# Issuing the y matmuls of a recurrence as two matmuls of 64 tokens each, in two column groups of the TensorE array

## The chip, the cores and the metric

One core of a Trainium2 chip runs the whole kernel. The metric is the device time of one execution in microseconds (us); the median of three runs of the kernel before is 934.26 us (932.96 to 934.57). TensorE multiplies matrices, VectorE and ScalarE work on vectors and evacuate results from PSUM, GpSimd does small jobs, and SyncE issues the transfers. A matmul here has a stationary operand, loaded into the array (its columns become the rows of the result), and a moving operand that is streamed through it.

## The reference, cut to what matters

```python
# 4 batches x 8 heads, 768 tokens, 48 features per head
for t in range(S):
    state = alpha[:, :, t, :, None] * state + np.einsum('bhd,bhe->bhde', k[:, :, t], v[:, :, t])
    y[:, :, t] = np.einsum('bhd,bhde->bhe', q[:, :, t], state)
# heads side by side: x is 3072 x 384
xn = x / sqrt(mean(x * x) + 1e-6) * rms_g
x = (silu(xn @ w_gate) * (xn @ w_val)) @ w_out          # d_ff = 1536
out = max(x @ w1, x @ w2, x @ w3) @ w_out2              # d_ff = 768
```

## The kernel before

The recurrence is cut into 24 tiles of 128 tokens of one batch: six chunks of four batches, so tiles 0 to 3 have no state yet, tiles 4 to 23 do, and tiles 20 to 23 are the last chunk, which leaves no state. Heads are treated in four pairs. For a tile, VectorE turns the inputs (in tiles 0 to 5 TensorE does), makes running products of alpha in a first half (`pre_br`) and in a second half (`pre_bq`), and writes kT, qT and the decayed state Sd. TensorE then forms the scores of each head (`pe_b`, line 643, two groups of rows of the array), VectorE masks them into `at`, and `pe_c` makes from them U, the tile's own contribution to the state (line 666), and y. U's two matmuls of a pair write partitions 0 to 47 and 64 to 111. y has a matmul with the state for both heads of a pair (line 673, 96 moving columns) and one with `at` for each head (line 678, 48 moving columns); each has all 128 tokens as columns of its stationary operand. All of these are float32, and each appears in the trace as two loads and two matmuls. Then y is normalized, turned (line 712) and split into two float32r halves, xh and xl.

The first MoE goes over the 3072 tokens in eight blocks of 384 (three tiles) and over the hidden layer in strips of 128: one block with one strip is a slot, and there are 96. A slot has a gate (`g`, line 756), an up-projection (`v`, line 756) and a down-projection (`s`, line 803), of nine matmuls of 128x384 each; VectorE multiplies the two (line 789, "the product" of the slot), which frees the PSUM bank for the next slot's up-projection, and splits the result (line 797). The first two blocks take turns, so that strips 0 to 5 of the weights are first used in slots 0 to 5, and strips 6 to 11 in slots 12 to 17. The weights are float64; VectorE joins their words (lines 57 to 59) and splits them in two (line 379), two chunks of 128x384 at a time. The second MoE follows; its weights are loaded once the last tile is through.

All of this is one program order, written by a planner (`Order`): each part has an engine, a cost, a due slot and parts that it needs, and the planner plays this through once, starting on each engine the due part that can start. What it writes per engine is then executed in that order. Until the first up-projection it adds fillers to TensorE where it expects rest, products that nothing uses (line 763). Each engine executes its own list in order and waits on semaphores for the others.

Of the kernel before, what the change touches and what calls it, by code (L numbers as in the profile page):

```python
# [37 lines left out]
# The upper word of a float64, read as a float32, grows with the number's magnitude. From  # L38
# 2**-119 to 2**121 it is in [LEAST, MOST).
# [6 lines left out]
def words(raw, n):  # L46
    """Upper words (as bits and as float32) and lower words of n float64s."""
    bits, floats = (raw.bitcast(t).rearrange("p (n w) -> p n w", w=2) for t in (I32, F32))
    return bits[:, :n, 1], floats[:, :n, 1], bits[:, :n, 0]


def join(nc, raw, t, n):
    """Float64 to float32 bits, in three steps: sign, exponent and the first 23 bits of the mantissa,
    the last of them set (its error is then as often up as down)."""
    up, _, low = words(raw, n)
    bits = t.bitcast(I32)
    yield nc.vector.tensor_scalar(bits, up, 3, TOP2 + 1, ALU.logical_shift_left, ALU.bitwise_or)
    yield nc.vector.scalar_tensor_tensor(bits, up, BELOW, bits, ALU.bitwise_or, ALU.bitwise_and)  # L58
    yield nc.vector.scalar_tensor_tensor(bits, low, 29, bits, ALU.logical_shift_right, ALU.bitwise_or)  # L59


def any_weight(nc, p, dst, src, n):
    """float64 to float32 of any magnitude: what is too small becomes 0, what is too large inf."""
    raw = p.tile([P, n], I64, name="aw_raw")
    nc.sync.dma_start(out=raw, in_=src)
    up, upf, low = words(raw, n)
    sq = p.tile([P, n], F32, name="aw_sq")
    nc.vector.tensor_tensor(sq, upf, upf, ALU.mult)
    small = p.tile([P, n], I32, name="aw_small")
    nc.vector.tensor_scalar(small, sq, LEAST * LEAST, -1.0, ALU.is_ge, ALU.mult)  # L70
    large = p.tile([P, n], I32, name="aw_large")
    nc.vector.tensor_scalar(large, sq, MOST * MOST, -1.0, ALU.is_ge, ALU.mult)
    e = p.tile([P, n], F32, name="aw_e")
    for _ in join(nc, raw, e, n):
        pass
    bits = e.bitcast(I32)
    nc.vector.tensor_tensor(bits, bits, small, ALU.bitwise_and)
    inf = p.tile([P, n], I32, name="aw_inf")
    nc.vector.tensor_scalar(inf, up, SIGN, 0x7F800000, ALU.bitwise_and, ALU.bitwise_or)
    nc.vector.copy_predicated(bits, large.bitcast(U32), inf)  # L80
    nc.vector.tensor_copy(dst, e)


def slow_path(ctx, tc, q, k, v, alpha, wg, wv, wo, g, w1, w2, w3, wo2, out, x_scr):
    """The recurrence as it stands, then both MoEs in float32 products."""
# [91 lines left out]
class Order:  # L177
    """The order in which the parts of the kernel are issued. Each part occupies one engine for
    about its cost and needs other parts done; of those that can start, the one due first does.
    Some hold PSUM banks until other parts are done."""  # L180

    SIGNAL = 0.1
    # The tensor engine runs at half its clock in a tick if fewer than ENOUGH columns left it in the last.
# [13 lines left out]
    def busy_tensor(self, t, cost, columns):  # L197
        """When the tensor engine, from t on, is through with what takes it cost at its full clock."""
        while cost > 1e-9:
            tick = int(t / self.TICK + 1e-9)  # L200
            slow = 1 if self.count.get(tick - 1, 0) >= self.ENOUGH else 2
            step = min(cost, ((tick + 1) * self.TICK - t) / slow)
            self.count[tick] = self.count.get(tick, 0) + columns * step / cost
            columns -= columns * step / cost
            cost -= step
            t += step * slow
        return t
# [73 lines left out]
def gla_moe_moe(ctx: ExitStack, tc: tile.TileContext, q, k, v, alpha, wg, wv, wo, g, w1, w2, w3, wo2, out):  # L281
# [35 lines left out]
    # LAT: from a load's issue until its data can be used; HEAD: slots by which the first chunks are ahead.  # L317
# [3 lines left out]
    class Weights:  # L321
        """Float64 weights loaded ahead, then cut into two float32r, two chunks at a time."""

        def __init__(self, tag, pool, bufs, chunks, where, due, needs):
            """chunks: source and shape; where(i): the two destinations; due(i): slot of first use."""
# [57 lines left out]
        def check(self, i):  # L383
            """Magnitudes outside of float32's normal range make sums that are too large."""
# [10 lines left out]
        def ready(self, i):  # L395
            """What has to be done before chunk i is used."""
            return (self.tag, "rest", i - i % 2)

# [1 line left out]
    # The first two blocks take turns, so that each weight is used twice as it comes.  # L400
# [54 lines left out]
    def take(n, rows, a, w):  # L455
        """A bank that nothing waits in, the one free for the longest."""
# [15 lines left out]
    # The tensor engine turns the operands of the first tiles, while the vector engine is the busier one.  # L472
    NPE = 6

    class Tile_:
        """One tile of 128 tokens."""

        def __init__(self, n):
# [4 lines left out]
            # Slots of the first MoE by which its parts are due: at + step * (0 to 4).  # L483
# [40 lines left out]
            add("pc", "PE", (2.57 if c else 1.72) + (0 if last else 0.5), 2.5,  # L524
# [12 lines left out]
        def load(self):  # L537
# [7 lines left out]
            # Partition 64 j + 32 u + t of an input's tile: tokens 4 t to 4 t + 3 of the heads of parity  # L545
            # j, from feature 32 u on (and, past a token's last feature, what nothing uses).
# [26 lines left out]
        def turn(self, dst, src):  # L573
            """Features to the partitions (those of a head to 0 to 47 or 64 to 111), tokens along them."""
# [12 lines left out]
        def pre_br(self):  # L587
            # R[s]: product of alpha after s; Q[t]: product up to t over the whole tile's.
            # One scan over the four pairs: a zero multiplier starts each anew.
# [70 lines left out]
        def pe_c(self):  # L660
            vt, at = self.vt, self.at
            if self.c < NC - 1:
                self.U, self.in_u = take(self.n, W, NP, D)
                for pr in range(NP):
                    for i, lo, hi in HALVES:
# [3 lines left out]
                        )  # L669
            self.y, self.in_y = take(self.n, P, H, D)  # L670
            for pr in range(NP):
                if self.c:
                    nc.tensor.matmul(  # L673
                        self.y[:, 2 * pr:2 * pr + 2, :].rearrange("p a d -> p (a d)"), self.qT[:, pr, :],
                        Sds[self.s][:, pr, :], start=True, stop=False, skip_group_check=True,
                    )
                for i in range(2):
                    nc.tensor.matmul(  # L678
                        self.y[:, 2 * pr + i, :], at[i][:, pr, :], vt[:, 2 * pr + i, :],
                        start=not self.c, stop=True, skip_group_check=True,  # L680
                    )
# [79 lines left out]
    def fill():  # L761
        """A product that nothing uses: the tensor engine's clock falls when it rests."""
# [231 lines left out]
    def flag():  # L994
        """1 if all operands were in the range of the chunked form and of the split weights."""
# [50 lines left out]
```

## Time and profile before

| | |
|---|---|
| median of the runs | 934.26 us (932.96 to 934.57) |
| span of the profiled execution, from its first to its last instruction | 932.6 us |
| TensorE busy with matmuls | 904.6 us, 97% of the span |
| TensorE busy with loads of stationary operands | 884.9 us, 95% |
| VectorE busy | 528.1 us, 57% |
| ScalarE busy | 352.5 us, 38% |

The page's time of the profiled execution is its span; the timed runs are told by the device and lie a little above. Loads run beside matmuls, so the first two shares overlap. The ends of matmuls are modelled, and one is drawn longer than its place in the stream: how long a run of them takes is read from start to start. The share of VectorE is an average: the page's 40 slices show it at eight or nine tenths and more from the second to the eighth and at three or less at the end.

### The profile page before, as it was taken

What the parts mean: (1) busy time and instruction counts of PE and PEld (TensorE: products, weight loads), DVE (VectorE), ACT (ScalarE), POOL (GpSimd) and SP (SyncE); (2) the same over time, 40 slices, a digit from 0 to 9 for tenths busy, and PEclk for the clock granted to TensorE, in tenths of its full rate; (3) what the DMA queues carried; (4) which work ended last, traced back from release to release, by engine and by line L of the source; (5) the groups of instructions that cost most, each with busy time, mean ns of one, the idle gap of its engine ahead of it and who ended that gap; (6) DMA issues with size and microseconds to landing.
All of it is one profiled execution on the core that took longest, in us unless ns stands there. A gap on an engine that the chain in (4) does not pass through costs nothing.

```text
span 932.6 us, 15178 instructions
## 1 busy us (share of the span) xinstructions
PE 904.6 (97%) x5910; PEld 884.9 (95%) x5910; DVE 528.1 (57%) x1052; ACT 352.5 (38%) x898; POOL 23.2 (2%) x70
## 2 busy tenths in 40 slices
PE   4899999999999999999999999999999999999997
PEld 3798999999999999999999999999999999999996
DVE  3989999987666666666666347556323323323221
ACT  3567777323233323233223258644212212212121
POOL 1000000000000000000000000000000000000000
PEclk9989999999999999999999999999999999999999
DMA  8746646343122122223221026321100101101000
GB/s 169 146 115 179 175 141 188 84 117 87 43 55 73 45 51 78 56 56 81 56 56 53 1 75 180 102 92 45 52 26 26 51 1 51 32 21 51 1 26 29
DMA packets 106238, 69.08 MB, mean 74 GB/s; under 512 B 49200, under 2 KB 103856, under 8 KB 106160
## 3 DMA queue, kind: packets, MB, share of 16 engines
q1 hardware_dynamic: 106160, 68.05, 27.5%
q8 instruction: 48, 0.79, 0.4%
q14 instruction: 30, 0.25, 0.1%
HBM read 57.41 MB, written 10.62 MB: 73 GB/s over the span
## 4 chain that ended last, share of the span: by engine, by line
PE 88%; DVE 5%; DMA 3%; issue 2%; ACT 1%; POOL 0%; SPq 0%; DVEq 0%; POOLq 0%; ACTq 0%
PE bank L756 53%; PE bank L803 15%; PE bank L956 8%; PE bank L678 4%; PE bank L673 2%; PE bank L643 2%; DMA raw<-in_moe_w_dram 2%; PE bank L666 1%; PE bank L712 1%; DVE cv_t L58 1%; PE bank L569 1%; DVE R L597 1%; PE bank L636 1%; PE bank L763 1%; DVE cv_t L59 1%
## 5 line engine op out<-in xcount | busy, mean ns | idle before, releaser
L941 DVE TENSOR_TENSOR sg<-sg,bank 128x384 f32<-128x384 f32 x96 | 53.1, 554 | 172.0 <-PE bank L756 165.6
L789 DVE TENSOR_TENSOR sg<-sg,bank 128x384 f32<-128x384 f32 x96 | 53.0, 552 | 107.8 <-PE bank L756 107.7
L793 ACT ACTIVATE hh<-sg 128x384 fp32r<-128x384 f32 x96 | 50.2, 523 | 144.0 <-DVE sg L789 144.0
L756 PE MATMUL bank<-xh,wgh 128*128 128x384 f32 x288 | 100.3, 348 | 0.0
L756 PE MATMUL bank<-xh,wvh 128*128 128x384 f32 x288 | 97.0, 337 | 1.6 <-DVE sg L789 1.4
L803 PE MATMUL bank<-hh,woh 128*128 128x384 f32 x288 | 98.1, 341 | 0.0
L803 PE MATMUL bank<-hl,woh 128*128 128x384 f32 x288 | 96.5, 335 | 0.2 <-DVE hl L797 0.2
L756 PE MATMUL bank<-xl,wgh 128*128 128x384 f32 x288 | 96.6, 335 | 0.0
L756 PE MATMUL bank<-xh,wgl 128*128 128x384 f32 x288 | 96.5, 335 | 0.0
L756 PE MATMUL bank<-xh,wvl 128*128 128x384 f32 x288 | 96.4, 335 | 0.0
L803 PE MATMUL bank<-hh,wol 128*128 128x384 f32 x288 | 96.4, 335 | 0.0
L756 PE MATMUL bank<-xl,wvh 128*128 128x384 f32 x288 | 96.3, 334 | 0.0
L945 ACT ACTIVATE hh<-sg 128x384 fp32r<-128x384 f32 x48 | 25.2, 525 | 160.3 <-DVE sg L941 160.3
L797 DVE TENSOR_TENSOR hl<-sg,hh 128x384 fp32r<-128x384 f32 x96 | 53.2, 554 | 31.9 <-ACT hh L793 31.8
L786 ACT ACTIVATE sg<-bank 128x384 f32<-128x384 f32 x96 | 46.8, 487 | 55.0 <-PE bank L756 54.9
L756 PEld LDWEIGHTS bank<-xh,wvh 128*128 128x128 f32 x288 | 54.1, 188 | 3.0 <-DVE sg L789 2.8
L803 PEld LDWEIGHTS bank<-hh,woh 128*128 128x128 f32 x288 | 54.0, 188 | 1.7
L678 PE MATMUL bank<-vt,at 128*128 128x48 f32 x384 | 55.2, 273 | 0.0
L756 PEld LDWEIGHTS bank<-xh,wgh 128*128 128x128 f32 x288 | 54.2, 188 | 0.9 <-ACT sg L786 0.2
L803 PEld LDWEIGHTS bank<-hl,woh 128*128 128x128 f32 x288 | 54.1, 188 | 0.5 <-DVE hl L797 0.5
L756 PEld LDWEIGHTS bank<-xl,wgh 128*128 128x128 f32 x288 | 54.2, 188 | 0.0
L756 PEld LDWEIGHTS bank<-xh,wgl 128*128 128x128 f32 x288 | 54.1, 188 | 0.0
(137 smaller groups left out, 2049.1 us busy)
## 6 DMA issues: line engine op xcount, KB each, us to landing
raw<-in_moe_w_out_dram SPq DMA_DIRECT2D x18, 384.0 KB, 3.8
raw<-in_moe_w_dram SPq DMA_DIRECT2D x18, 384.0 KB, 3.9
y_scr<-yo SPq DMA_DIRECT2D x30, 192.0 KB, 2.3
raw<-in_moe_w_gate_dram SPq DMA_DIRECT2D x12, 384.0 KB, 4.3
vt<-in_v_dram SPq DMA_DIRECT2D x24, 192.0 KB, 3.0
raw<-in_moe_w_val_dram SPq DMA_DIRECT2D x12, 384.0 KB, 3.7
xl<-y_scr SPq DMA_DIRECT2D x8, 576.0 KB, 4.4
out_dram<-yo SPq DMA_DIRECT2D x24, 192.0 KB, 2.0
```

Source lines behind the costliest of these rows:

```text
L643: nc.tensor.matmul(self.sc[i][:, pr, :], self.kT[lo:hi, pr, :], self.qT[lo:hi, pr, :], start=True, stop=True)
L673: nc.tensor.matmul(self.y[:, 2 * pr:2 * pr + 2, :].rearrange("p a d -> p (a d)"), self.qT[:, pr, :], Sds[self.s][:, pr, :], start=True, st ...
L678: nc.tensor.matmul(self.y[:, 2 * pr + i, :], at[i][:, pr, :], vt[:, 2 * pr + i, :], start=not self.c, stop=True, skip_group_check=True,)
L756: nc.tensor.matmul(ps, w_[:, kt, col], m_[:, kt, :], start=i == 0, stop=i == 3 * KT - 1)
L786: nc.scalar.activation(hid[s], banks[3][:, :NB], AF.Silu)
L789: nc.vector.tensor_tensor(hid[s], hid[s], banks[4][:, :NB], ALU.mult)
L793: nc.scalar.activation(hi_[s], hid[s], AF.Copy)
L797: nc.vector.tensor_tensor(lo_[s], hid.pop(s), hi_[s].bitcast(F32), ALU.subtract)
L803: nc.tensor.matmul(banks[e][:, :NB], w_[:, f, es], m_, start=f == f0 and i == 0, stop=f == f1 - 1 and i == 2)
L941: nc.vector.tensor_tensor(hid2[z], hid2[z], banks[3 + j][:, :NB], ALU.max)
L945: nc.scalar.activation(hi2[z], hid2[z], AF.Copy)
L956: nc.tensor.matmul(banks[t][:, :DM], l_[:, tsl], r_[:, f, :], start=f == 0 and i == 0, stop=f == NF2 - 1 and i == 2)
```

## The change

Each matmul of y is issued as two, for tokens 0 to 63 and 64 to 127: the columns of the stationary operand and the partitions of the result are halved, the moving operand stays. The two write partitions 0 to 63 and 64 to 127, so they stand in two groups of 64 columns of the array, and they are issued in turn. The planner's cost of the part that holds them (`pc`) is lowered. Comments are removed elsewhere, and lines move by up to four.

```diff
+TOKENS = slice(0, 64), slice(64, 128)
...
-            add("pc", "PE", (2.57 if c else 1.72) + (0 if last else 0.5), 2.5,
+            add("pc", "PE", (1.4 if c else 0.9) + (0 if last else 0.5), 2.5,
...
             for pr in range(NP):
                 if self.c:
-                    nc.tensor.matmul(
-                        self.y[:, 2 * pr:2 * pr + 2, :].rearrange("p a d -> p (a d)"), self.qT[:, pr, :],
-                        Sds[self.s][:, pr, :], start=True, stop=False, skip_group_check=True,
-                    )
+                    for tk in TOKENS:
+                        nc.tensor.matmul(
+                            self.y[tk, 2 * pr:2 * pr + 2, :].rearrange("p a d -> p (a d)"), self.qT[:, pr, tk],
+                            Sds[self.s][:, pr, :], start=True, stop=False, skip_group_check=True,
+                        )
                 for i in range(2):
-                    nc.tensor.matmul(
-                        self.y[:, 2 * pr + i, :], at[i][:, pr, :], vt[:, 2 * pr + i, :],
-                        start=not self.c, stop=True, skip_group_check=True,
-                    )
+                    for tk in TOKENS:
+                        nc.tensor.matmul(
+                            self.y[tk, 2 * pr + i, :], at[i][:, pr, tk], vt[:, 2 * pr + i, :],
+                            start=not self.c, stop=True, skip_group_check=True,
+                        )
```

The lower cost makes the planner write another order up to slot 18; from there on VectorE's and TensorE's lists are the same but for the matmuls themselves. On TensorE, U and the first pair of y of a tile with a state stood so before, and so now (each name reads result<-moving,stationary with the shape of the result; x8 counts equal rows in a run):

```order
L756 MATMUL bank_77<-xh,wvl 128x384
L666 MATMUL bank_78<-vt,kn 48x48 x8
L673 MATMUL bank_79<-Sd_117,qT 128x96
L678 MATMUL bank_79<-vt,at 128x48 x2
L673 MATMUL bank_79<-Sd_117,qT 128x96
```

```order
L760 MATMUL bank_77<-xh,wvl 128x384
L667 MATMUL bank_78<-vt,kn 48x48 x8
L676 MATMUL bank_79<-Sd_117,qT 64x96 x2
L682 MATMUL bank_79<-vt,at 64x48 x4
L676 MATMUL bank_79<-Sd_117,qT 64x96 x2
```

Twice as many y matmuls stand there, of half the rows; U is as it was. On VectorE, around the product of slot 8 (the last row but two before, the last but one after; `R` and kT are the first half of a tile's preparation, `starts` to qT the second) stood and stands:

```order
L602 TENSOR_SCALAR least<-R 112x4
L603 TENSOR_TENSOR kT<-kT,R 112x512
L789 TENSOR_TENSOR sg<-sg,bank_77 128x384
L379 TENSOR_TENSOR wol<-cv_t,woh 128x384
L379 TENSOR_TENSOR wgl<-cv_t,wgh 128x3x128
L797 TENSOR_TENSOR hl<-sg,hh 128x384
L57 TENSOR_SCALAR cv_t<-raw 128x384 x2
L58 SCALAR_TENSOR_TENSOR cv_t<-raw,cv_t 128x384 x2
L59 SCALAR_TENSOR_TENSOR cv_t<-raw,cv_t 128x384 x2
L789 TENSOR_TENSOR sg<-sg,bank_77 128x384
L607 RECIPROCAL starts<-least 112x4
L609 TENSOR_TENSOR all<-all,least 112x4
```

```order
L603 TENSOR_SCALAR least<-R 112x4
L604 TENSOR_TENSOR kT<-kT,R 112x512
L801 TENSOR_TENSOR hl<-sg,hh 128x384
L380 TENSOR_TENSOR wol<-cv_t,woh 128x384
L380 TENSOR_TENSOR wgl<-cv_t,wgh 128x3x128
L608 RECIPROCAL starts<-least 112x4
L610 TENSOR_TENSOR all<-all,least 112x4
L611 SCALAR_TENSOR_TENSOR aT<-aT,starts 112x512
L617 TENSOR_TENSOR Sd_118<-S_128,all 48x4x48 x2
L621 TENSOR_TENSOR qT<-qT,aT 112x512
L793 TENSOR_TENSOR sg<-sg,bank_77 128x384
L58 TENSOR_SCALAR cv_t<-raw 128x384 x2
```

The second half of a tile's preparation has moved ahead of this product, and a weight join behind it; further up, a whole preparation has moved ahead as well. Farther on in VectorE's list, ahead of the last split of gate weights (wgl, which the gate of slot 17 uses first), stood and stands:

```order
L57 TENSOR_SCALAR cv_t<-raw 128x384 x2
L58 SCALAR_TENSOR_TENSOR cv_t<-raw,cv_t 128x384 x2
L59 SCALAR_TENSOR_TENSOR cv_t<-raw,cv_t 128x384 x2
L789 TENSOR_TENSOR sg<-sg,bank_77 128x384
L575 STREAM_TRANSPOSE aT<-in_al 128x4x4x32
L575 STREAM_TRANSPOSE kT<-in_kk 128x4x4x32
L575 STREAM_TRANSPOSE qT<-in_qq 128x4x4x32
L797 TENSOR_TENSOR hl<-sg,hh 128x384
L379 TENSOR_TENSOR wol<-cv_t,woh 128x384
L379 TENSOR_TENSOR wgl<-cv_t,wgh 128x3x128
```

```order
L60 SCALAR_TENSOR_TENSOR cv_t<-raw,cv_t 128x384 x2
L801 TENSOR_TENSOR hl<-sg,hh 128x384
L793 TENSOR_TENSOR sg<-sg,bank_77 128x384
L608 RECIPROCAL starts<-least 112x4
L610 TENSOR_TENSOR all<-all,least 112x4
L611 SCALAR_TENSOR_TENSOR aT<-aT,starts 112x512
L617 TENSOR_TENSOR Sd_117<-S_125,all 48x4x48 x2
L621 TENSOR_TENSOR qT<-qT,aT 112x512
L380 TENSOR_TENSOR wol<-cv_t,woh 128x384
L380 TENSOR_TENSOR wgl<-cv_t,wgh 128x3x128
```

Tile 8's two halves, which stood behind this split, now stand ahead of it. On TensorE, the down-projection of slot 15 has moved ahead of the gate of slot 17, and that of slot 16 ahead of tile 7's U. The lists count 118 fillers before and 141 now.

## Rows read from the trace of the kernel before

**Rows 1.** Busy us (x instructions) by stretch: PE, PEld, DVE, ACT, POOL; clock.
```profile
20.00:176.70 156.70, 150.05 (x1142) 142.35 (x1139) 149.66 (x323) 105.71 (x301) 7.01 (x16) 0.98 0.57 148
...
200.00:540.00 340.00, 340.00 (x2371) 331.45 (x2370) 203.32 (x378) 102.94 (x257) 11.12 (x30) 1.00 0.24 59
```
**Rows 2.** Order of time around slot 19: start us, us, engine, line [idle <- releaser].
```profile
176.09 0.55 DVE L789 TENSOR_TENSOR sg<-sg,bank 128x384 f32<-128x384 f32 x1
...
176.70 0.45 PE L756 MATMUL bank<-xh,wvh 128*128 128x384 f32 x1 [0.60 <-DVE sg L789]
```
**Rows 3.** TensorE in order of time: y of tile 9, y of tile 20.
```profile
201.71 0.46 PE L673 MATMUL bank<-Sd,qT 112*128 112x96 f32 x2
...
204.41 0.42 PE L803 MATMUL bank<-hh,woh 128*128 128x384 f32 x1
...
464.99 0.36 PE L673 MATMUL bank<-Sd,qT 112*128 112x96 f32 x2
...
467.59 0.42 PE L756 MATMUL bank<-xh,wgh 128*128 128x384 f32 x1
```
**Rows 4.** TensorE's loads in order of time, tile 9: scores, next gate, U, Sd, vt.
```profile
198.33 0.97 PEld L643 LDWEIGHTS bank<-qT,kT 48*128 48x128 f32 x16
199.43 0.19 PEld L756 LDWEIGHTS bank<-xh,wgh 128*128 128x128 f32 x1
...
201.22 0.44 PEld L666 LDWEIGHTS bank<-vt,kn 128*48 128x48 f32 x16 [0.25 <-issue]
201.71 0.30 PEld L673 LDWEIGHTS bank<-Sd,qT 112*128 112x128 f32 x2
...
203.94 0.53 PEld L678 LDWEIGHTS bank<-vt,at 128*128 128x128 f32 x4
```
**Rows 5.** One load by itself, by line: ns minimum/median/maximum, over the whole span.
```profile
L643 PEld LDWEIGHTS bank<-qT,kT x384: 182/188/188, 20.4 to 530.8; 48*128 48x128 f32 x192
...
L666 PEld LDWEIGHTS bank<-vt,kn x320: 119/125/198, 23.4 to 441.6; 128*48 128x48 f32 x160
```
**Rows 6.** VectorE in order of time: transposes, first half and second half of tile 9.
```profile
170.12 1.09 DVE L575 STREAM_TRANSPOSE aT<-in_al 128x512 f32<-128x512 f32 x1
...
172.92 0.54 DVE L723 TENSOR_TENSOR xl<-bank,xh 128x384 fp32r<-128x384 f32 x1
...
173.84 0.15 DVE L594 COPY all<-aT 112x4 f32<-112x4 f32 x1
...
177.03 0.17 DVE L607 RECIPROCAL starts<-least 112x4 f32<-112x4 f32 x1
...
179.70 0.55 DVE L797 TENSOR_TENSOR hl<-sg,hh 128x384 fp32r<-128x384 f32 x1
```
**Rows 7.** Order of time: product of slot 8, slot 9; last gate split, slot 17.
```profile
116.20 0.55 DVE L789 TENSOR_TENSOR sg<-sg,bank 128x384 f32<-128x384 f32 x1
...
118.02 0.33 PE L756 MATMUL bank<-xh,wvh 128*128 128x384 f32 x1
...
157.50 0.53 DVE L379 TENSOR_TENSOR wgl<-cv_t,wgh 128x384 fp32r<-128x384 f32 x1
...
159.26 0.44 PE L756 MATMUL bank<-xh,wgh 128*128 128x384 f32 x1
```
**Rows 8.** The chain that ended last: a down-projection's nine products, start us, us.
```profile
161.10 1.56 PE bank L803 x9
```
**Rows 9.** Order of time around y of tile 2, TensorE and VectorE.
```profile
46.35 3.65 PE L678 MATMUL bank<-vt,at 128*128 128x48 f32 x16
...
51.62 0.62 DVE L706 SCALAR_TENSOR_TENSOR xn<-bank,r,gb 128x384 f32<-128x384 f32 x1 [2.29 <-POOL r L692]
...
55.43 0.56 DVE L723 TENSOR_TENSOR xl<-bank,xh 128x384 fp32r<-128x384 f32 x1 [0.94 <-ACT xh L719]
```
**Rows 10.** TensorE before tile 2's U, and the stretch of the lower clock.
```profile
45.66 0.76 PE L666 MATMUL bank<-vt,kn 128*48 128x48 f32 x16 [2.47 <-issue]
...
45.90:52.80 6.90, 6.90 (x46) 6.67 (x41) 4.48 (x13) 3.66 (x12) 0.74 (x2) 0.51 0.24 56
```

## The prediction

> **What bounds the kernel now.** I read the page's shares and slices first, then busy time by stretch, then single waits. The page shows TensorE busy almost throughout, so time taken from it can come off the end; where it can is told by the stretches. From 200 to 540 us TensorE is busy for all 340.00 us, VectorE for 203.32: TensorE alone bounds. From 20 to 176.7 us VectorE is busy for 149.66 of 156.70 us, so both engines are full, and a saving on TensorE buys nothing there unless VectorE's 7.0 us of rest shrink [rows 1]. The two stages meet at 176.70 us, where the up-projection of slot 19 waited 0.60 us for VectorE's product of slot 18, which begins at 176.09 [rows 2]. So I sum in two parts: tiles 8 to 23, after that meeting, where TensorE sets the pace, and all that lies before it, where VectorE's order decides.
>
> **What y costs now.** Each float32 matmul leaves two records. A tile with a state has 8 records with Sd and 16 with vt in y and takes 204.41 - 201.71 = 2.70 us; a last-chunk tile takes 467.59 - 464.99 = 2.60 [rows 3]. The loads show what sets this. Four loads of y's 128 columns take 0.53 us together; one such load lasts 0.19 (the scores' 0.188), so one begins every (0.53 - 0.19)/3 = 113 ns. Sd's two begin (0.30 - 0.19) = 110 ns apart, though they stream 96 columns instead of 48 [rows 4, 5]. At full width the load sets the round, and the stream hides under it. U, in the same function, already alternates between two column groups: 16 loads of 48 columns in 0.44 us, 0.125 for the last, which makes 8 rounds of 45 ns with two records in each [rows 4, 5]. That is what the change asks of y, with the same vt streamed over 128 partitions, so I take the two groups as concurrent.
>
> **What it costs after.** From 48 columns (45 ns) to 128 (113) the slope is 0.85 ns per column; 64 columns give 45 + 16 x 0.85 = 58 ns. Each matmul becomes two of half the width, in one round per record: 16 rounds of vt, 0.93 us. Sd streams 96 columns, and no row shows that beside so short a load. Its round lies between 58 ns (stream still hidden) and 110 (today's). The nearest row is the scores: 16 records in two row groups stream 128 columns in 8 rounds of (0.97 - 0.188)/7 = 112 ns [rows 4, 5]; if the stream sets that round, 96 columns need 84. I take 84: 8 rounds, 0.67 us. The Trainium skill (FP8 and Floating Point Precision, TensorE Precision Notes) counts four passes for a true FP32 product; over two records that makes 96 columns stream for 80 ns, an estimate from that page. If the rule did not hold here, Sd's round would be 58 and a tile 0.21 us shorter; no run so far shows which.
>
> y then takes 1.60 us, 1.10 less. Entering and leaving the split is not free. After the scores the next load begins 199.43 - 199.30 = 0.13 us past the end of the last score load, where loads in a run overlap by 0.08 (0.125 - 0.045): leaving costs 0.21. U to Sd has such a seam now (0.05 us of gap, 0.13 with the overlap lost), and it goes [rows 4]. Net 0.08: 1.02 us saved per tile with U. The four last-chunk tiles have no U and pay for both ends: 2.60 - 1.60 - 0.21 - 0.13 = 0.66. Tiles 8 to 19: 12 x 1.02 = 12.2. Tiles 20 to 23: 4 x 0.66 = 2.6. Together 14.8 us. TensorE's order around these tiles is the same as before, and no wait takes their place: VectorE rests 40% of the time from 200 to 540 us [rows 1], and the weight loads of the second MoE begin when the last tile is done, so the waits for them move along. With Sd's round at 58 ns the sum is 18.2, at 110 it is 11.5.
>
> **The stretch up to slot 19.** The planner's cost for this part fell by 1.17 us (0.82 without a state), so the orders differ. (1) There are 141 fillers in place of 118, which use up TensorE's early saving. (2) VectorE now has, ahead of the products of slots 5 to 10, the whole preparation of one more tile: three transposes (2.80 us), a first half (2.25) and a second half (2.67), 7.7 us [rows 2, 6]; ahead of slot 8's it is another second half more and one weight join less, which about cancel. The product of slot 8 ends at 116.75 today, and the up-projection of slot 9, which overwrites the bank that it reads, starts at 118.02 [rows 7]. (3) Against this VectorE gets back some rest. It waited 2.29 us for the norm of tile 2, whose y took 3.65 us at half clock and should take about 1.9 plus its end, 1.6 less; and 0.94 us before a subtraction behind which other work stands now [rows 9]. That is 2.5 us of the 7.0. So the product of slot 8 ends at 116.75 + 7.7 - 2.5 = 121.95, and slot 9 starts 3.9 us later than today. TensorE has no rest from there to the gate of slot 17 and carries this on: 159.26 + 3.9 - 1.02 (tile 6) + 1.56 (the nine products of slot 15's down-projection, which now stand ahead of that gate) = 163.7 [rows 7, 8]. (4) This gate's weights are ready at 158.03 today and have a first half, a second half and a product (0.55), 5.5 us, more ahead of them; less 2.5, that is 161.0, so they don't bind [rows 6, 7]. (5) From that gate to slot 19 it was 17.44 us; without the 0.60 of waiting, without that down-projection and with tile 7's y shorter by 1.02 it is 14.26: 178.0 instead of 176.70. Forecast for the stretch: 1.3 us lost, and tiles 0 to 7 give nothing. If VectorE gets back no rest, 3.8 lost; if all 7.0, about 3.2 won; never more than 0.60 + 4 x 1.02 = 4.7, TensorE's own saving since tile 4.
>
> **Sum.** 14.8 - 1.3 = 13.5 us. The profiled execution's span is 932.6 us; the median of the timed runs, 934.26, lies 1.7 above, and I take that to stay: 920.8.
>
> **Rivals.**
> A. Sd's stream stays hidden, its round is 58 ns. For it: today 96 and 48 columns cost the same. Against: the load that hides them gets half as long. 3.4 more: 917.4.
> B. The new order on VectorE costs nothing, and the stretch wins 4.7. For it: nearly half of VectorE's rest there is the two waits of [rows 9]. Against: 7.7 us stand ahead of a product with 1.3 of slack. 6.0 more: 914.8.
> C. The new wait before slot 9 lets the clock fall. For it: after 2.47 us of rest before tile 2's U the granted clock went from the upper level, 2.4 GHz, to the lower, 1.2, for 6.9 us (mean 0.51) [rows 10]. Against: the wait may come in pieces. Half of 6.9 is 3.4: 924.2.
> D. Slower: within a group the stream does not run under the next load. A round is then load plus stream, 5 + (64 + 48) x 0.85 = 100 ns for vt and 141 for Sd: 2.73 us per tile against 2.70, and with the seams 12 x 0.11 + 4 x 0.47 + 1.3 = 4.5 us slower, 938.8. It decides from a mean round of (2.70 - 0.08)/24 = 109 ns on. Against: by this sum U's round would be 86 ns, and it is 45 [rows 4]. The Trainium skill (TensorE: Matmul & The Clock Gate, Part 3: Packing small matmuls — row/col tiling, The mechanism) has weight loads overlap running matmuls only where the row group differs, and these two groups share all rows. By that rule D holds; the trace of U disagrees.
>
> **Chances.** Forecast 0.50, A 0.19, B 0.13, C 0.13, D 0.05. A measurement of this kernel tells no change from one within about 0.2%, 1.9 us. Forecast, A, B and C are all well past that; of D I put 0.02 within it. Faster 0.94, same 0.02, slower 0.04 (rounded). The forecast's own range is 917 to 925: the stretch from 3.2 won to 3.8 lost. The whole range takes in A, C and most of B: 912 to 927.
>
> **What would show it.** In the profile after: loads 64 columns wide, twice as many with vt and with Sd, about 29 ns apart; y of a tile in 1.6 us (1.4 is A, 2.7 or more D); a wait of TensorE of some 4 us for VectorE's product of slot 8 or a neighbour near 118 us (none is B); slot 19 near 178 us. I am wrong if a tile's y is outside 1.4 to 1.8 us, or if slot 19 starts outside 173 to 181.

## The result, and the profile after

The changed kernel takes 926.28 us (median of 4 runs, 925.15 to 927.95) against 934.11 us for the kernel before beside it (932.96 to 934.57): a ratio of 0.9919, 95% interval 0.9900 to 0.9938, so 7.8 us faster. 920.8 was predicted. The profiled execution spans 925.2 us, 7.4 less than the 932.6 of before. Lines are four later than before (L760 for L756, L793 for L789, L807 for L803); U, Sd's and vt's matmuls are L667, L676 and L682.

The matmuls themselves came out as worked out. TensorE in order of time, tile 8 (start us, us, engine, line, operation, result<-moving,stationary) and the last-chunk tile 20:

```profile
193.87 0.56 PE L667 MATMUL bank<-vt,kn 128*48 128x48 f32 x16
194.26 0.35 PE L676 MATMUL bank<-Sd,qT 112*64 112x96 f32 x4
194.45 0.39 PE L682 MATMUL bank<-vt,at 128*64 128x48 f32 x8
194.66 0.35 PE L676 MATMUL bank<-Sd,qT 112*64 112x96 f32 x4
...
195.97 0.44 PE L760 MATMUL bank<-xh,wgh 128*128 128x384 f32 x1
...
460.69 0.34 PE L760 MATMUL bank<-xh,wvl 128*128 128x384 f32 x1
460.96 0.39 PE L676 MATMUL bank<-Sd,qT 112*64 112x96 f32 x4
...
462.69 0.44 PE L760 MATMUL bank<-xh,wgh 128*128 128x384 f32 x1
```

Read from start to start. A pair of heads takes 194.66 - 194.26 = 0.40 us, a tile's four pairs 1.60. From the start of y to the next product it is 195.97 - 194.26 = 1.71 us where it was 2.70 (tile 9 of [rows 3]), and in tile 20 it is 462.69 - 460.96 = 1.73 where it was 2.60 [rows 3]. U to Sd takes 0.39 where it took 0.49 [rows 4]. Tile 20 has no U and enters the split from a product of 128 columns. Entering takes 460.96 - 460.69 = 0.27 us. Before, y began 464.99 - 464.82 = 0.17 us after this row:

```profile
464.82 0.34 PE L756 MATMUL bank<-xh,wvl 128*128 128x384 f32 x1
```

So tiles 8 to 19 save 0.99 + 0.10 = 1.09 us each, tiles 20 to 23 save 0.87 - 0.10 = 0.77: 12 x 1.09 + 4 x 0.77 = 16.2.

The stretch before them went wrong. Slot 19's up-projection, TensorE in order of time:

```profile
185.83 0.33 PE L760 MATMUL bank<-xh,wvh 128*128 128x384 f32 x1
```

It began at 176.70 [rows 2]. From there to the end it was 932.6 - 176.7 = 755.9 us and is 925.2 - 185.8 = 739.4: 16.5 saved. Up to there 9.1 were lost. Busy time by stretch (PE, PEld, DVE, ACT, POOL, then granted clock), of the changed kernel:

```profile
20.00:185.80 165.80, 150.07 (x1328) 139.84 (x1326) 151.88 (x326) 108.22 (x304) 8.20 (x16) 0.95 0.53 142
...
97.00:117.00 20.00, 13.52 (x48) 12.69 (x49) 17.92 (x38) 11.87 (x33) 0.00 (x0) 0.66 0.55 147
117.00:140.00 23.00, 23.00 (x134) 22.95 (x133) 18.46 (x43) 16.17 (x46) 0.00 (x0) 1.00 0.55 178
```

VectorE did 151.88 us of work up to slot 19, 2.2 more than the 149.66 of [rows 1], and rested 13.9 us in place of 7.0: 2.2 + 6.9 = 9.1. The two lower rows show where. From 97 to 117 us TensorE works 13.52 of 20.00 us; then it is full to the last and VectorE rests 4.5 us in 23. The same two stretches of the kernel before had both engines full:

```profile
97.00:117.00 20.00, 20.00 (x119) 19.97 (x118) 19.70 (x45) 15.07 (x41) 0.48 (x1) 1.00 0.69 189
117.00:140.00 23.00, 23.00 (x144) 22.53 (x142) 22.47 (x49) 16.32 (x47) 0.00 (x0) 1.00 0.49 138
```

What stopped TensorE after 97 us, in order of time (the bracket is the idle time before the row, and what ended it):

```profile
98.81 0.69 PE L760 MATMUL bank<-xh,wvh 128*128 128x384 f32 x1 [2.80 <-ACT wvh L374]
...
101.46 0.69 PE L760 MATMUL bank<-xh,wvl 128*128 128x384 f32 x1 [1.64 <-DVE wvl L380]
...
109.06 0.69 PE L760 MATMUL bank<-xh,wvh 128*128 128x384 f32 x1 [3.03 <-DVE sg L793]
```

These are the up-projections of slots 5 and 6: slot 5 waits for both halves of its weights, slot 6 for slot 5's product. VectorE in order of time there:

```profile
92.97 0.55 DVE L801 TENSOR_TENSOR hl<-sg,hh 128x384 fp32r<-128x384 f32 x1
93.43 1.09 DVE L576 STREAM_TRANSPOSE aT<-in_al 128x512 f32<-128x512 f32 x1
...
96.23 0.59 DVE L58 TENSOR_SCALAR cv_t<-raw 128x384 int32<-128x384 int32 x2
...
98.59 0.16 DVE L595 COPY all<-aT 112x4 f32<-112x4 f32 x1
...
103.62 0.36 DVE L58 TENSOR_SCALAR cv_t<-raw 128x384 int32<-128x384 int32 x1 [1.47 <-DMA raw<-in_moe_w_val_dram]
...
105.77 0.17 DVE L608 RECIPROCAL starts<-least 112x4 f32<-112x4 f32 x1
...
108.46 0.55 DVE L793 TENSOR_TENSOR sg<-sg,bank 128x384 f32<-128x384 f32 x1
```

Between slot 4's low part (92.97) and slot 5's product (108.46) stands the whole preparation of tile 6, transposes from 93.43, first half from 98.59, second half from 105.77, and between its pieces the joins of slot 5's weights (96.23) and of a later strip's, which waited 1.47 us for a transfer. I call that a bundle below.

### The profile page after: what moved, and what is told of

Read it like the earlier page. It is cut to its first block, busy times and chain, and to the rows that moved or that the text cites. A ratio compares the mean times of both kernels' runs of the same rounds, so it can differ in the third digit from the quotient of the medians.

```text
span 925.2 us, 16299 instructions
## 1 busy us (share of the span) xinstructions
PE 888.6 (96%) x6477; PEld 864.7 (93%) x6477; DVE 527.4 (57%) x1052; ACT 353.4 (38%) x898; POOL 24.3 (3%) x70
## 4 chain that ended last, share of the span: by engine, by line
PE 84%; DVE 7%; DMA 2%; ACT 1%; issue 1%; POOL 0%; SPq 0%; DVEq 0%; POOLq 0%; ACTq 0%
PE bank L760 53%; PE bank L807 14%; PE bank L960 8%; PE bank L644 2%; PE bank L682 2%; PE bank L676 2%; DMA raw<-in_moe_w_dram 1%; DMA raw<-in_moe_w_val_dram 1%; PE bank L667 1%; DVE cv_t L59 1%; PE bank L716 1%; DVE aT L611 1%; DVE cv_t L60 1%; PE bank L637 1%; DVE sg L793 1%
## 5 line engine op out<-in xcount | busy, mean ns | idle before, releaser
L793 DVE TENSOR_TENSOR sg<-sg,bank 128x384 f32<-128x384 f32 x96 | 52.8, 551 | 104.2 <-PE bank L760 103.5
L760 PE MATMUL bank<-xh,wvh 128*128 128x384 f32 x288 | 98.7, 343 | 7.3 <-DVE sg L793 4.3
L760 PE MATMUL bank<-xh,wgh 128*128 128x384 f32 x288 | 100.8, 350 | 0.0
L760 PE MATMUL bank<-xh,wvl 128*128 128x384 f32 x288 | 97.7, 339 | 1.6 <-DVE wvl L380 1.6
L760 PE MATMUL bank<-xh,wgl 128*128 128x384 f32 x288 | 97.2, 337 | 1.5 <-DVE wgl L380 1.5
L807 PE MATMUL bank<-hh,woh 128*128 128x384 f32 x288 | 98.5, 342 | 0.0
L807 PE MATMUL bank<-hl,woh 128*128 128x384 f32 x288 | 96.7, 336 | 1.8 <-DVE hl L801 1.8
L760 PE MATMUL bank<-xl,wvh 128*128 128x384 f32 x288 | 97.4, 338 | 0.0
L760 PE MATMUL bank<-xl,wgh 128*128 128x384 f32 x288 | 97.1, 337 | 0.0
L807 PE MATMUL bank<-hh,wol 128*128 128x384 f32 x288 | 96.4, 335 | 0.0
L760 PEld LDWEIGHTS bank<-xh,wvh 128*128 128x128 f32 x288 | 54.8, 190 | 9.8 <-DVE sg L793 6.4
L760 PEld LDWEIGHTS bank<-xh,wvl 128*128 128x128 f32 x288 | 54.9, 191 | 2.2 <-DVE wvl L380 2.2
L807 PEld LDWEIGHTS bank<-hl,woh 128*128 128x128 f32 x288 | 54.1, 188 | 2.7 <-DVE hl L801 2.7
L760 PEld LDWEIGHTS bank<-xh,wgl 128*128 128x128 f32 x288 | 54.6, 190 | 1.8 <-DVE wgl L380 1.8
L807 PEld LDWEIGHTS bank<-hh,woh 128*128 128x128 f32 x288 | 54.2, 188 | 2.0
L760 PEld LDWEIGHTS bank<-xh,wgh 128*128 128x128 f32 x288 | 54.8, 190 | 1.3
L760 PEld LDWEIGHTS bank<-xl,wvh 128*128 128x128 f32 x288 | 54.9, 191 | 0.0
```

Source lines behind the costliest of these rows:

```text
L760: nc.tensor.matmul(ps, w_[:, kt, col], m_[:, kt, :], start=i == 0, stop=i == 3 * KT - 1)
L793: nc.vector.tensor_tensor(hid[s], hid[s], banks[4][:, :NB], ALU.mult)
L807: nc.tensor.matmul(banks[e][:, :NB], w_[:, f, es], m_, start=f == f0 and i == 0, stop=f == f1 - 1 and i == 2)
```

## Experiments

Starts (us) of the up-projections of some slots, read in each profiled execution, what lies from slot 19 to the end of it, and the median time of the runs:

| kernel | 5 | 7 | 16 | 17 | 19 | 19 to end | median us |
|---|---|---|---|---|---|---|---|
| before | 99.2 | 108.7 | 156.1 | 165.8 | 176.7 | 755.9 | 934.1 |
| changed | 98.8 | 116.6 | 163.3 | 176.9 | 185.8 | 739.4 | 926.28 |
| changed, again | 98.5 | 115.8 | 164.1 | 177.6 | 186.6 | 739.8 | 927.77 |
| 1: split, old order | 96.2 | 105.7 | 152.1 | 160.6 | 173.3 | 740.8 | 916.25 |
| 2: old matmuls, new order | 103.9 | 120.8 | 168.2 | 182.8 | 191.8 | 755.1 | 948.51 |
| 3: gates issued again | 98.6 | 114.9 | 162.4 | 175.9 | 184.9 | 740.8 | 926.78 |
| 4: cost as measured | 98.1 | 112.9 | 159.8 | 173.4 | 182.3 | 741.2 | 925.03 |
| 5: tiles 6 and 9 held | 98.5 | 107.2 | 156.6 | 172.3 | 183.0 | 740.0 | 921.85 |
| 6: tile 6 held | 98.6 | 107.4 | 157.3 | 173.1 | 186.6 | 739.5 | 926.42 |
| 7: old order, tile 6 early | 95.0 | 109.3 | 158.1 | 165.0 | 176.5 | 743.7 | 921.94 |
| 8: no alternation | 97.5 | 107.0 | 154.8 | 164.8 | 175.3 | 761.7 | 939.12 |
| 9: Sd streams 48 | 96.7 | 106.1 | 152.3 | 160.7 | 173.8 | 737.7 | 913.72 |

Theory: the matmuls save what was worked out, and the order that the planner makes from the lower cost loses the rest before slot 19. Rival: a faster TensorE disturbs that stretch by itself.

**1. The split matmuls in the old order.** Of the changed kernel only the planner's cost goes back:

```diff
-            add("pc", "PE", (1.4 if c else 0.9) + (0 if last else 0.5), 2.5,
+            add("pc", "PE", (2.57 if c else 1.72) + (0 if last else 0.5), 2.5,
```

> The matmuls of y are split as in the changed kernel, but the planner reckons with the old cost of a y, so that every engine has the order of the kernel before. Theory (the 9.1 us lost before product slot 19 come from the order that the lower cost makes): slot 19's product starts at 173 to 177 us as before, the 16.5 us saved after it stay, and the time is 915 to 918 us. Rival (a faster TensorE disturbs that stretch whatever the order): slot 19 at about 186 us and some 926 us, as the changed kernel.

916.25 us (5 runs, 914.77 to 916.75), ratio to before 0.9802, interval 0.9781 to 0.9823: this version beats both kernels. Slot 19 starts at 173.30, and from there to the end 15.1 us are saved (755.9 - 740.8), not all of the 16.5. Busy time by stretch:

```profile
20.00:173.30 153.30, 143.90 (x1303) 134.13 (x1301) 150.62 (x326) 106.13 (x301) 8.02 (x16) 0.98 0.60 153
...
105.70:128.50 22.80, 22.80 (x133) 22.80 (x133) 22.62 (x50) 16.82 (x48) 0.00 (x0) 1.00 0.69 190
```

VectorE rests 2.7 us in 153.3, and from slot 7 to slot 12 both engines are full. VectorE in order of time shows the same preparation spread out: slot 5's product, transposes, first half, slot 8's product, second half.

```profile
99.14 0.55 DVE L793 TENSOR_TENSOR sg<-sg,bank 128x384 f32<-128x384 f32 x1
99.60 1.09 DVE L576 STREAM_TRANSPOSE aT<-in_al 128x512 f32<-128x512 f32 x1
...
107.12 0.16 DVE L595 COPY all<-aT 112x4 f32<-112x4 f32 x1
...
113.67 0.54 DVE L793 TENSOR_TENSOR sg<-sg,bank 128x384 f32<-128x384 f32 x1
114.13 0.17 DVE L608 RECIPROCAL starts<-least 112x4 f32<-112x4 f32 x1
```

The rival falls: with the same matmuls, the order alone is worth 10 us (11.5 against the changed kernel run beside it, 927.77).

**2. The old matmuls in the new order.** The kernel before, with the lower cost:

```diff
-            add("pc", "PE", (2.57 if c else 1.72) + (0 if last else 0.5), 2.5,
+            add("pc", "PE", (1.4 if c else 0.9) + (0 if last else 0.5), 2.5,
```

> The y matmuls are those of the kernel before, 128 tokens each, but the planner reckons with the changed kernel's lower cost, which gives the changed kernel's order. Theory (the order loses the 9.1 us): slot 19's product at 185 to 190 us, nothing saved after it, 942 to 947 us. Rival (the order costs nothing): slot 19 at 176 to 178 us and about 934 us, the time of the kernel before.

948.51 us (4 runs, 948.02 to 950.53), ratio 1.0156, interval 1.0130 to 1.0182. Slot 19 was at 191.8, and both this and the time are later than either theory had them; from slot 19 to the end it took 755.1 us, near the 755.9 of before. The order by itself costs 14 us on these matmuls.

**3. Without a fall of the clock.** The waits of 2.80 and 3.03 us above lie where the granted clock went to its lower level, 1.2 GHz. Busy time by stretch of the changed kernel, clock third from the end:

```profile
97.50:104.40 6.90, 3.94 (x11) 3.44 (x12) 5.29 (x14) 3.00 (x9) 0.00 (x0) 0.53 0.88 226
107.80:114.70 6.90, 5.64 (x18) 5.64 (x19) 6.87 (x14) 4.96 (x15) 0.00 (x0) 0.53 0.20 51
```

The changed kernel, with work to fill the rests:

```diff
+    AGAIN = {5: 2, 6: 3}
...
-            products(banks[3][:, :NB], (wgh, wgl), (xh[blk], xl[blk]), cols(f))
+            for _ in range(AGAIN.get(s, 1)):
+                products(banks[3][:, :NB], (wgh, wgl), (xh[blk], xl[blk]), cols(f))
```

> The changed kernel, with the gate matmuls of slot 5 issued twice and those of slot 6 three times into the same bank (the same result again), which fill TensorE's rests between 88 and 104 us. Theory (the two falls of the clock at 97.5 and 107.8 us cost about half of what is lost before slot 19): the clock stays at its upper level from 97 to 115 us, slot 7's product starts near 114 us in place of 116.6, and the time is 921 to 924 us. Rival (VectorE, with the strip's splits ahead of the products, sets this stretch alone): no gain, 926 us or more.

926.78 us (6 runs, 925.13 to 930.49; ratio 0.9923, interval 0.9899 to 0.9947), against 927.77 for the changed kernel beside it: no difference that these runs can tell. Its clock by stretch:

```profile
104.00:108.00 4.00, 4.00 (x16) 4.00 (x16) 3.97 (x10) 2.77 (x8) 0.00 (x0) 0.58 0.47 172
108.00:115.00 7.00, 7.00 (x41) 6.80 (x41) 6.99 (x13) 5.66 (x17) 0.00 (x0) 1.00 0.31 75
```

Only the second fall went; the first stayed, since slot 5's up-projection still waits for its weights. Slot 7 is 0.9 to 1.7 us earlier than in the two runs of the changed kernel, and that stays to slot 19. So the second fall costs a us or two, and the 921 to 924 us of the theory did not come; what the first fall costs alone was not separated. The changed kernel, run again:

> The changed kernel once more, beside the other runs on the same chip: 926 us, slot 19's product at 185 to 187 us, by either theory.

It took 927.77 us (6 runs, 925.98 to 928.26), ratio 0.9923, interval 0.9904 to 0.9942.

**4. A cost as the trace has it.**

```diff
-            add("pc", "PE", (1.4 if c else 0.9) + (0 if last else 0.5), 2.5,
+            add("pc", "PE", (1.65 if c else 0.97) + (0 if last else 0.45), 2.5,
```

> The changed kernel with the planner's cost of a y set to what the changed kernel's trace shows (1.65 and 0.97, and 0.45 for U) in place of 1.4, 0.9 and 0.5. The order it makes still puts a whole preparation of tile 6 between the products of slots 4 and 5. Theory (what counts is where the preparations stand on VectorE, not whether the cost is true): slot 19's value matmuls start at 182 to 188 us and the time is 922 to 930 us. Rival (a cost too low is the fault, and a true one mends it): slot 19 at 173 to 177 us and 915 to 918 us.

925.03 us (4 runs, 924.57 to 925.48; ratio 0.9888, interval 0.9860 to 0.9916), slot 19 at 182.31. The true cost makes nearly the same bundle. The old cost, now about 1 us too high (2.57 + 0.5 against 1.65 + 0.45), gives the better order, not because it is true but, as experiments 5 to 7 suggest, by where it lets the preparations fall.

**5 and 6. The bundle held back.** The changed kernel, with needs added ahead of the planner's run; experiment 6 has the first line only.

```diff
+    for late, held_by in ((("t", "bt", 6), ("mu", 5)), (("t", "br", 6), ("hl", 6)), (("t", "b", 6), ("mu", 8)),
+                          (("t", "bt", 9), ("mu", 17)), (("t", "br", 9), ("hl", 17)), (("t", "b", 9), ("mu", 18))):
+        plan.parts[late][3].append(held_by)
```

> The changed kernel with its low cost, and six added needs in the planner: tile 6's transposes wait for the product of slot 5, its first half for the low part of slot 6, its second half for the product of slot 8, and tile 9's three likewise for slots 17, 17 and 18; that is where the order of before has them. Theory (VectorE's bundle of tile 6's preparation between the products of slots 4 and 5 costs the 8 us there): slot 5's value matmuls start at 96 to 99 us, slot 7's 9.5 to 11 us after them in place of 17.8, slot 19's at 174 to 179 us, and the time is 915 to 920 us. Rival (the loss is spread over the many other places where the order differs): slot 7 later than 112 us and 923 us or more.

921.85 us (4 runs, 921.36 to 924.77; ratio 0.9854, interval 0.9826 to 0.9882). Slots 5 to 7 did what the theory says, and a little more: slot 7 starts 8.8 us after slot 5 in place of 17.8, at 107.2 in place of 116.6. But slot 19 came at 183.0 and the time at 921.85, both later than I expected. Slot 17 is 15.7 us after slot 16 (156.6), and VectorE shows why, in order of time: the products of slots 16 and 17.

```profile
159.51 0.55 DVE L793 TENSOR_TENSOR sg<-sg,bank 128x384 f32<-128x384 f32 x1
...
161.38 0.17 DVE L595 COPY all<-aT 112x4 f32<-112x4 f32 x1
...
164.40 0.18 DVE L608 RECIPROCAL starts<-least 112x4 f32<-112x4 f32 x1
...
167.09 0.62 DVE L58 TENSOR_SCALAR cv_t<-raw 128x384 int32<-128x384 int32 x2
...
175.57 0.55 DVE L793 TENSOR_TENSOR sg<-sg,bank 128x384 f32<-128x384 f32 x1 [2.30 <-PE bank L760]
```

Here tile 8's first half (161.38), its second half (164.40) and a join of weights (167.09) stand together: a second bundle. The changed kernel has one at the same place: it takes 13.6 us from slot 16 to slot 17 (163.3 to 176.9), the kernel before 9.7 and experiment 1 8.6. Holding tile 6 left this one standing and made it 2.1 us longer. So the loss sits in two places, which neither the theory nor its rival had. Whether my needs on tile 9 had done that was the next question.

> As the run with tiles 6 and 9 held, but only tile 6's three needs are added; tile 9's preparation stands where the planner puts it, and two second halves, a first half and a mask now stand between the products of slots 16 and 17. Theory (a bundle on VectorE between two products delays the later one wherever it stands): slot 7's value matmuls at 106 to 109 us again, slot 17's 15 to 18 us after slot 16's, and 921 to 926 us. Rival (in the run before it was tile 9's added needs that made slot 17 late): slot 17's 8 to 11 us after slot 16's and 915 to 918 us.

926.42 us (4 runs, 923.90 to 928.37; ratio 0.9912, interval 0.9877 to 0.9946), just above the 921 to 926 expected. Slot 7 again at 107.4, slot 17 again 15.8 us after slot 16: not the needs on tile 9. The bundle at slot 5 costs about 9 us there, and holding it alone wins nothing in the end: from slot 7 to slot 16 (157.3) the run takes 3 us more than the changed kernel (163.3 - 116.6), and from there to slot 19 another 7.

**7. The bundle alone, in the old order.** Experiment 1, with tile 6 due early:

```diff
+    for kind, due in (("bt", 4.5), ("br", 4.5), ("b", 4.5)):
+        p = plan.parts["t", kind, 6]
+        plan.parts["t", kind, 6] = p[:2] + (due,) + p[3:]
```

> The split matmuls with the old cost and the order of before (the run of 916.25 us), with one difference asked of the planner: tile 6's transposes, first and second half are due at slot 4.5 in place of 13, which puts all of them between the products of slots 4 and 5. Theory (that bundle is the loss): slot 5's product 4 to 6 us later than in that run, slot 7's value matmuls at 110 to 114 us in place of 105.7, little of it given back by slot 19 (177 to 181 us), and a time of 920 to 924 us. Rival (the bundle is harmless alone, VectorE does the same work sooner): slot 19 within 1.5 us of 173.3 and 915 to 918 us.

921.94 us (4 runs, 921.51 to 923.62; ratio 0.9861, interval 0.9831 to 0.9891), 5.7 more than experiment 1. Slot 5's product begins at 103.27 where it began at 99.14, 4.1 us later as expected; slot 7 is 3.6 us later and slot 19 3.2, each just short of what I had named (110 and 177), and little of it is given back. Some of the other parts moved too, since the planner plays the whole order anew. Another 2.9 us lie behind slot 19 (743.7 after 740.8), and its trace shows two more bundles there. At 256.26 and at 303.76 an up-projection waits for VectorE's product, the first so:

```profile
256.26 0.44 PE L760 MATMUL bank<-xh,wvh 128*128 128x384 f32 x1 [1.09 <-DVE sg L793]
```

Ahead of each of these two products a first half and a second half stand together (from 250.72 and from 298.22). Experiment 1 has a product between the first such two (at 249.75) and no wait at either place; from slot 31 to slot 35 and from slot 39 to slot 43 it takes 1.4 us longer here than there, each time.

So the bundle of tile 6 costs here too, but about 4 us where the changed kernel loses 9 at the same place. The changed kernel has joins of weights inside the bundle and this one has none; that this makes the difference in size is not shown.

**8. No alternation.** Experiment 1, with the loop over the two halves of the tokens outermost:

```diff
-            for pr in range(NP):
-                if self.c:
-                    for tk in TOKENS:
...
+            for tk in TOKENS:
+                for pr in range(NP):
+                    if self.c:
...
```

> The split matmuls with the order of before, but within a tile all y matmuls of tokens 0 to 63 are issued first and then all of tokens 64 to 127, so that neighbours stand in the same column group. Theory (the gain is that a matmul of one column group runs beside the load and the stream of the other's): a tile's y takes 2.6 to 3.4 us in place of 1.60, and the time goes to 930 to 942 us. Rival (the gain is only that a load of 64 columns is half as long): 1.6 us a tile and 915 to 918 us.

939.12 us (one run). TensorE in order of time, tile 9:

```profile
200.59 0.34 PE L676 MATMUL bank<-Sd,qT 112*64 112x96 f32 x2
...
200.99 0.34 PE L676 MATMUL bank<-Sd,qT 112*64 112x96 f32 x2
...
201.79 0.34 PE L676 MATMUL bank<-Sd,qT 112*64 112x96 f32 x2
201.97 0.21 PE L681 MATMUL bank<-vt,at 128*64 128x48 f32 x1
201.98 0.30 PE L676 MATMUL bank<-Sd,qT 112*64 112x96 f32 x1
...
202.41 0.34 PE L676 MATMUL bank<-Sd,qT 112*64 112x96 f32 x2
...
203.71 0.45 PE L806 MATMUL bank<-hh,woh 128*128 128x384 f32 x1
```

A pair now takes 0.40 us for one half of the tokens, as long as for both in turn before; y takes 203.71 - 200.59 = 3.12 us, more than the 2.70 of the unsplit form. Only where the halves meet do rows of Sd and vt mix, and there two pairs pass in 202.41 - 201.79 = 0.62 us in place of 0.80. So neighbours run side by side only when they stand in different column groups; a load half as long by itself gains nothing here.

**9. A shorter stream for Sd.** Experiment 1, with:

```diff
-                            self.y[tk, 2 * pr:2 * pr + 2, :].rearrange("p a d -> p (a d)"), self.qT[:, pr, tk],
-                            Sds[self.s][:, pr, :], start=True, stop=False, skip_group_check=True,
+                            self.y[tk, 2 * pr, :], self.qT[:, pr, tk],
+                            Sds[self.s][:, pr, 0:D], start=True, stop=False, skip_group_check=True,
...
-                            start=not self.c, stop=True, skip_group_check=True,
+                            start=not self.c or i == 1, stop=True, skip_group_check=True,
```

The last two lines let vt's matmul of the second head begin that head's result, since no matmul with Sd does so any more.

> The split matmuls with the order of before; the matmuls against Sd stream 48 columns in place of 96 (the state's part of y is left out for the second head of each pair). Theory (the round of two Sd matmuls takes 0.09 us because of its 96 streamed columns): it falls to 0.05 to 0.06 us, a tile's y from 1.60 to 1.25 to 1.35 us, and the time to 910 to 914 us. Rival (the load, or the first accumulation into the bank, sets it): 0.09 us and 1.60 us as before, 915 to 918 us.

913.72 us (one run). TensorE in order of time:

```profile
197.72 0.29 PE L676 MATMUL bank<-Sd,qT 112*64 112x48 f32 x4
197.83 0.40 PE L682 MATMUL bank<-vt,at 128*64 128x48 f32 x8
198.06 0.29 PE L676 MATMUL bank<-Sd,qT 112*64 112x48 f32 x4
...
199.22 0.44 PE L807 MATMUL bank<-hh,woh 128*128 128x384 f32 x1
```

Sd's two rounds go from 0.19 us to 0.11 or 0.12 with the same load of 64 columns, and y to the next product from 1.71 to 1.50 us. The theory holds in the round; the tile saved 0.2 us and not the 0.25 to 0.35 I expected, since vt's four rounds grew from 0.21 to 0.23; why they grew was not looked into.

## Why the prediction was right, and where it missed

The time, 926.28 us, is 5.5 above the forecast: outside its own range of 917 to 925, inside the whole one of 912 to 927. Up to slot 19 it lost 7.8 us more than forecast (9.1 - 1.3); 1.7 came back after it (16.5 - 14.8), and 0.6 because the median lay 1.1 above the profiled span and not 1.7. So the way of the change and the matmuls were foreseen, and the first stretch was not.

**y after the change: right.** 1.60 us was predicted and 1.60 measured. That the two agree so closely is luck, from two errors that cancel: Sd's round is 0.19/2 = 95 ns where I took 84, vt's 0.21/4 = 52 where I took 58. That Sd's round is set by its stream was the choice against rival A, and experiment 9 shows it. The Trainium skill (FP8 and Floating Point Precision, TensorE Precision Notes) counts four passes for a true FP32 product, which gave an estimate of 80 ns for 96 columns. The 95 measured lies above that estimate, and far from the 58 that the load alone would give; with 48 columns (experiment 9) the round was 55 to 60 ns, about the load's 58.

**The net saving after slot 19: right, a little small.** 14.8 predicted, 16.5 measured. The terms that were off are the seams: I charged 0.21 for leaving the split and gave back 0.13 at its start. Measured, leaving costs 0.11 (1.71 - 1.60), and 0.10 comes back between U and Sd. That makes 1.09 per tile in place of 1.02, and 0.77 in place of 0.66 for the last chunk, which pays 0.13 for leaving and 0.10 for entering: 16.2 in all.

That this is so near to 16.5 is partly luck. Up to slot 79, which starts behind the last tile's y, the trace shows 15.0 saved (540.15 - 176.70 = 363.45 us before, 534.28 - 185.83 = 348.45 now). I had said that no wait would take the place of the time saved; two up-projections, at 471.55 and 494.57, now wait 0.45 us each for VectorE's product. The other 1.5 came behind slot 79, where no y is left, and where a wait of 0.84 us for VectorE in the kernel before (at 584.04) is gone. Experiment 1 has 14.7 and 0.4 in their place.

**Rival D: refuted**, by 1.60 us in place of 2.73. Experiment 8 speaks against its premise too: there two records with Sd and four with vt follow each other in one column group in 0.40 us, and load plus stream would be 2 x 141 + 4 x 100 ns = 0.68. The Trainium skill (TensorE: Matmul & The Clock Gate, Part 3: Packing small matmuls — row/col tiling, The mechanism) has weight loads overlap running matmuls only where the row group differs. The trace disagrees: two groups of columns that share all rows took together, in turn, what one takes alone (0.40 us for a pair of heads).

**The stretch up to slot 19: this step failed.** 1.3 us lost was forecast and 9.1 measured, with slot 19 at 185.83, outside the 173 to 181 that I had named as the test. By its parts:

- Parts (2) and (3). I had VectorE's added work about right and its rest wrong. Busy time by stretch, up to slot 9, of the changed kernel and of the kernel before:

```profile
20.00:126.00 106.00, 93.47 (x885) 85.80 (x883) 99.10 (x215) 68.47 (x195) 6.54 (x12) 0.92 0.58 148
```

```profile
20.00:118.00 98.00, 91.95 (x745) 86.13 (x743) 92.37 (x202) 68.94 (x197) 5.30 (x12) 0.97 0.60 152
```

Slot 9 came 7.9 us later (125.95 after 118.02), not 3.9. VectorE works 6.7 us more ahead of it (I had 7.7) and rests 6.9 us in place of 5.6, where I had 2.5 less and 1.3 of slack at slot 8 to use up. The wait for tile 2's norm shrank as forecast, from 2.29 to 0.44, but new waits came. VectorE's waits from 20 to 185.8 us of the changed kernel (in total, times, longest):

```profile
DVE sg L793 <- PE bank L760: 4.5, 3, 2.3
DVE cv_t L58 <- DMA raw<-in_moe_w_val_dram: 3.0, 2, 1.5
DVE xn L710 <- POOL r L696: 1.3, 2, 0.9
```

The waits for products of 1.8 and 2.3 us lie at 118.42 and 137.17, behind the bundle, where TensorE is full and VectorE ahead of it. Of the two waits for transfers one is in the bundle (103.62), the other at 152.16. I read both as weights joined late, which leave their raw buffers to be refilled late; no run shows that. I looked for the wait at slots 8 and 9 because I summed VectorE's work up to there; it came at slots 5 and 6, where the work stands.

- Part (4) said that the gate of slot 17 would not wait for its weights. It did (weights ready at 170.2 and not at 161.0), and the down-projection behind it waited for its low part. TensorE in order of time:

```profile
170.24 0.44 PE L760 MATMUL bank<-xh,wgl 128*128 128x384 f32 x1 [1.53 <-DVE wgl L380]
...
173.18 0.44 PE L807 MATMUL bank<-hl,woh 128*128 128x384 f32 x1 [1.25 <-DVE hl L801]
```

With that, part (5) measured 185.83 - 168.20 = 17.6 us from that gate to slot 19, where I had 14.26. From slot to slot, against the kernel before: the changed kernel loses 8.3 us from slot 5 to 7 and 4.0 from slot 16 to 17, and wins 3.2 elsewhere.

- What I did not reckon with at all is that the work VectorE does early is not paid back. From slot 9 to slot 19 it had 52.8 us to do in 59.8, before it was 57.3 in 58.7. TensorE's own work set the pace at first (23.00 of 23.00 us busy from 117 to 140), so the lead that VectorE had bought with the delay was spent resting; at slots 16 and 17 TensorE waited for VectorE again.

**Rival C happened, twice, with a smaller price.** The clock fell at 97.5 and 107.8, 6.9 us each. I had priced one such fall at 3.4 us; taking the second away moved slot 19 by 0.9 to 1.7 us and the time by nothing these runs can tell. **Rival B: refuted.** With the new order the stretch lost 9.1 us, and B had it win 4.7. It is the old order that wins there: experiment 1 gains 176.7 - 173.3 = 3.4 us, close to the 3.2 I gave for all rest regained. The order decided it, and I had read the order by sums instead of by what stands between each two products.

## What to carry to other kernels

Where two engines are both nearly full and wait for each other at every step, the sum of work ahead of a point said little here: look at the longest run of other work that stands between two neighbouring hand-overs, since what one engine lost there the other did not give back. When a planner writes the order, a change of a cost is a second change: run the new instructions in the old order and the old ones in the new, before either is credited. Of float32 matmuls that stream few columns (48 and 96 here), halve the 128 stationary columns and alternate two column groups; without the alternation the split was slower than none.

## What the runs showed of the hardware that was not expected

- Two float32 matmuls of 64 columns each in two column groups that share all rows take together what one takes alone: 0.40 us for a pair of heads in both halves of the tokens, or in one (experiment 8).
- Going from the 64-column form back to 128 columns cost 0.11 to 0.13 us (1.71 and 1.73 less 1.60); I had taken 0.21 from the scores. Going into it from 128 columns cost 0.10 (0.27 after 0.17, tile 20).
- Two stretches of 6.9 us with a mean granted clock of 0.53, each beginning within a rest of TensorE of 2.8 or 3.0 us, came in the changed kernel; in them a product of 128x384 started every 0.32 us in place of 0.17. Taking the second of these away gave back 0.9 to 1.7 us at slot 19, of the 18 x 0.15 = 2.7 by which its products were slower.
